# A two-layer linear-attention and MLP kernel: the first MLP block's layer norm scaled on ScalarE and turned through DRAM, six queries put off, constants moved to GpSimd

## The chip, the cores and the metric

The kernel runs on one core of one Trainium2 chip. The metric is the device time of one execution in microseconds (us); the profile's span is the part of an execution from the core's first to its last recorded instruction. Engines: PE is TensorE (PEld its weight loads), DVE is VectorE, ACT is ScalarE, POOL is GpSimd, SP is SyncE, which issues most DMAs here.

## What is computed

`x` has 2048 rows of 448 values. Two layers run one after the other with the same weights, and each adds a linear-attention block (16 heads of 28) and an MLP block to `x`:

```python
phi = lambda t: jnp.where(t > 0, t + 1, jnp.exp(t)) + 1e-6
def A(x):
    q, k, v = split(x @ wqkv)
    pq, pk = phi(q), phi(k)
    kv = einsum("bhsd,bhse->bhde", pk, v);  z = pk.sum(rows)
    o = einsum("bhqd,bhde->bhqe", pq, kv) / (einsum("bhqd,bhd->bhq", pq, z)[..., None] + 1e-6)
    return merge(o) @ wo
def B(x):
    return gelu_tanh(x @ w1 + b1) @ w2 + b2
x = x + A(layernorm(x)); x = x + B(layernorm(x))
x = x + A(layernorm(x)); x = x + B(layernorm(x))
```

`w1` is 448x1792, `w2` 1792x448. Everything is float32.

## The kernel before, in words

**Tiles.** The rows are cut into 16 tiles of 128, four tiles make a block. A matrix product is done in two halves: each operand is split into a rounded part and the rest (hi and lo, type fp32r), and hi·hi, hi·lo and lo·hi are accumulated in PSUM. A query or key projection of one tile (Q, K) is therefore eleven matmuls into one bank; so is `f`, the first MLP product of 128 of the 1792 columns for a whole block; `y` is the second one, four `u` (one per tile) of three matmuls.

**Order.** Nothing is scheduled at run time. The string ORDER lists operations as short tokens (`Q10` is query projection of tile 10, `:m` or `:acc` names a bank or an engine, `>` marks an operation of the next layer done early); each token emits its instructions, and every engine works through its own instructions in that order. SP's DMAs too go out in that order; a DMA also waits for the one that was issued eight before it. So the order of the string is the order of every queue.

**Layer norm.** `a` and `la` take a tile's mean and variance on DVE and add 1e-5 (`bve`); `ar` raises that to -0.5 on POOL (`brs`); `n` and `ln` scale the tile on DVE (line 361). The result must be transposed before a product over its 448 columns. There are two ways: on PE (`T`, `mT`: four transposes against an identity, line 390, into one bank), or *in squares*: DVE transposes 32x32 squares (`tu`, `pu`, `mu`, lines 398 and 399), the half block of two tiles is stored to DRAM (`st`, `ps`, `ms`, line 404) and read back with four loads that put the squares in place (`sp`, `pp`, `mp`, line 410). Either way ACT then casts the hi part (`xh`, `qh`, `yh`) and DVE subtracts to get lo (`xl`, `ql`, `yl`). Before the change the first MLP block of each layer (tiles 0 to 3, `ln lx mT yh yl`) goes through PE, the other three blocks in squares (`ln mu ms mp yh yl`).

**Attention.** Keys run first: `K`, phi (`ke` on ACT, `kp` on DVE), hi and lo (`kh`, `kl`), the sum over rows `za`, and `G` = xnᵀ·phi(k), four banks. Queries (`Q qe qp`) are stored to DRAM (`qs`) and read back later (`pl`), since their denominators need the sum over all keys. After the last G: `z` and `zb` (the key sum on all partitions), `dc` (its 1e-6 share per head), `gt` (G to SBUF), `kv`, `mask`, and `m`: four products with `wo` (hi `mh`, lo `ml`). Per query tile: `pz` multiplies by zb on POOL, `pd` sums per head, adds dc and inverts on DVE, `pm` scales; for tiles 0 to 3 `pT` turns on PE, and `o`, `oa`, `la` add the attention to the tile and take its statistics. `oc` does the same for the later tiles, in between the MLP's `f` and `y`.

**MLP.** `f` (PE), `g` (gelu, ACT), `gh` (ACT) and `gl` (DVE), `y` (PE), at the end of a block `ya` (DVE) and `ys` (DMA out). `lb` adds b2 on POOL.

**Around the change.** In layer 0 PE's order after the key phase was: K15 G13 G14 z G15 Q11 kv pT1 Q12 m3 pT0 m0 m1 m2 pT3 o0 pT2 o1 o2 mT0 o3 Q13 mT1 mT2 Q14 mT3 Q15 f0; in layer 1: K15 G13 G14 G15 Q10 z kv Q11 m0 m1 m3 pT1 m2 pT0 Q12 o0 pT2 o1 pT3 o2 mT0 o3 mT1 Q13 mT2 Q14 mT3 Q15 f0. At the layer boundary: f54 f55 y50 y51 y52 y53 y54 K0 y55 Q0 K1 Q1 G0 (K0 on, of layer 1).

PSUM has eight banks: four `acc` (G, then m, o, then y), two `h` (T, Q, f), two `m` (K, z, kv, pT, mT, oc).

## Time and profile before

| | us |
|---|---|
| median of 3 runs | 879.77 |
| lowest, highest | 879.72, 881.26 |
| the profiled execution, its whole time | 879.86 |
| its span | 878.1 |
| granted clock of TensorE, mean | 0.999 |

In the rows below, a group row reads: line, engine, operation, out<-in with shapes, count | busy us, mean ns of one | idle time of the engine just before them and what ended most of it. A row of the chain or a timeline begins with its start and its duration in us. Matmuls are pipelined: a matmul's duration is longer than the distance to the next one's start, so PE's work is counted by starts.

### The profile page before, as it was taken

How to read it: one execution, taken by the hardware profiler on the slowest of the kernel's cores; microseconds unless marked ns; L12 is line 12 of the kernel's file. 1: busy time of each engine (PE TensorE's matmuls, PEld its weight loads, DVE VectorE, ACT ScalarE, POOL GpSimd, SP SyncE). 2: the span in 40 equal slices, each digit the busy share in tenths (PEclk: the TensorE clock that was granted, in tenths of full speed). 3: DMA queues.
4: the chain of work that ended last, by engine and by line, in shares of the span. 5: the costliest groups of instructions: out<-in, count | busy, mean ns of one | idle time of the engine just before them, and what ended most of it. 6: DMA issues, size and time to landing. Idle time of an engine off the chain costs nothing.

```text
span 878.1 us, 11548 instructions
## 1 busy us (share of the span) xinstructions
PE 872.7 (99%) x4181; PEld 772.6 (88%) x4181; DVE 473.4 (54%) x972; ACT 336.4 (38%) x596; POOL 202.5 (23%) x239
## 2 busy tenths in 40 slices
PE   9999999999999999999999999999999999999998
PEld 7999988889888888888889898988888888888887
DVE  7886587357574343324378765954572743343112
ACT  6777634332323221424255653333233132223221
POOL 4665543123132011010023233130220220130000
PEclk9999999999999999999999999999999999999999
DMA  6575732541713124221064452333125142120101
GB/s 210 175 238 175 215 95 104 166 117 58 221 50 117 43 68 119 63 84 49 24 204 161 138 182 84 95 125 98 66 87 166 46 119 86 37 96 5 38 1 43
DMA packets 62762, 93.71 MB, mean 107 GB/s; under 512 B 8816, under 2 KB 57968, under 8 KB 62704
## 3 DMA queue, kind: packets, MB, share of 16 engines
q1 hardware_dynamic: 62400, 92.51, 33.3%
q8 instruction: 33, 0.54, 0.3%
q10 hardware_dynamic: 304, 0.46, 0.2%
q14 instruction: 25, 0.20, 0.1%
HBM read 55.65 MB, written 34.08 MB: 102 GB/s over the span
## 4 chain that ended last, share of the span: by engine, by line
PE 97%; DVE 1%; DMA 1%; ACT 0%; POOL 0%; SPq 0%; issue 0%; ACTq 0%; POOLq 0%
PE y L878 10%; PE y L877 10%; PE y L879 10%; PE hp L851 9%; PE hp L852 9%; PE hp L850 9%; PE hp L854 3%; PE hp L853 3%; PE G L618 2%; PE G L619 2%; PE G L617 2%; PE psq L543 2%; PE psq L545 2%; PE psq L544 2%; PE psk L543 2%; PE psk L544 2%
## 5 line engine op out<-in xcount | busy, mean ns | idle before, releaser
L869 DVE TENSOR_TENSOR gl<-g,gh 128x512 fp32r<-128x512 f32 x112 | 79.8, 720 | 193.8 <-ACT gh L211 193.5
L859 ACT ACTIVATE g<-hp,b1s 128x512 f32<-128x512 f32 x112 | 76.3, 688 | 228.8 <-PE hp L854 210.4
L878 PE MATMUL y<-w2l,gh 128*128 128x448 f32 x448 | 163.7, 365 | 0.0
L877 PE MATMUL y<-w2h,gh 128*128 128x448 f32 x448 | 163.6, 365 | 0.0
L879 PE MATMUL y<-w2h,gl 128*128 128x448 f32 x448 | 163.6, 365 | 0.0
L851 PE MATMUL hp<-XH,w1l 128*128 128x512 f32 x336 | 131.2, 391 | 0.0
L852 PE MATMUL hp<-XL,w1h 128*128 128x512 f32 x336 | 131.1, 390 | 0.0
L850 PE MATMUL hp<-XH,w1h 128*128 128x512 f32 x336 | 131.1, 390 | 0.0
L211 ACT CAST gh<-g 128x512 fp32r<-128x512 f32 x112 | 69.1, 620 | 155.6 <-PE y L878 144.1
L357 POOL TENSOR_TENSOR brs<-bve,mhalf 128x1 f32<-128x1 f32 x64 | 41.0, 642 | 318.9 <-DVE bve L351 318.9
L877 PEld LDWEIGHTS y<-w2h,gh 128*128 128x128 f32 x448 | 84.1, 188 | 8.3
L878 PEld LDWEIGHTS y<-w2l,gh 128*128 128x128 f32 x448 | 84.1, 188 | 7.9
L879 PEld LDWEIGHTS y<-w2h,gl 128*128 128x128 f32 x448 | 84.2, 188 | 6.6
L852 PEld LDWEIGHTS hp<-XL,w1h 128*128 128x128 f32 x336 | 63.1, 188 | 13.6
L851 PEld LDWEIGHTS hp<-XH,w1l 128*128 128x128 f32 x336 | 63.1, 188 | 11.9
L850 PEld LDWEIGHTS hp<-XH,w1h 128*128 128x128 f32 x336 | 63.1, 188 | 11.8
L716 POOL TENSOR_TENSOR pz<-pq,zb 128x448 f32<-128x448 f32 x32 | 37.8, 1184 | 70.2 <-DVE dn L721 43.6
L535 POOL TENSOR_TENSOR xnl<-x,xnh 128x384 fp32r<-128x384 f32 x32 | 33.7, 1052 | 81.6 <-ACT xnh L211 81.5
L428 DVE TENSOR_TENSOR XL<-sp,XH 128x512 fp32r<-128x512 f32 x50 | 36.7, 748 | 23.3 <-ACT XH L211 23.3
L795 DVE TENSOR_TENSOR x<-op,x 128x448 f32<-128x448 f32 x32 | 19.8, 618 | 49.3 <-PE op L789 48.5
L853 PE MATMUL hp<-XH,w1x 128*128 128x512 f32 x112 | 43.6, 389 | 0.0
L854 PE MATMUL hp<-XL,w1x 128*128 128x512 f32 x112 | 43.6, 389 | 0.0
(162 smaller groups left out, 1572.7 us busy)
## 6 DMA issues: line engine op xcount, KB each, us to landing
x<-in_A_x_dram SPq DMA_DIRECT2D x32, 224.0 KB, 4.0
pq_d<-eq SPq DMA_DIRECT2D x32, 224.0 KB, 2.8
pq<-pq_d SPq DMA_DIRECT2D x32, 224.0 KB, 3.2
x<-x_d SPq DMA_DIRECT2D x32, 224.0 KB, 3.8
sq_a<-sq SPq DMA_DIRECT2D x13, 512.0 KB, 3.0
sp<-sq_a SPq DMA_DIRECT2D x52, 128.0 KB, 3.0
sq_q<-sq SPq DMA_DIRECT2D x12, 512.0 KB, 2.9
sp<-sq_q SPq DMA_DIRECT2D x48, 128.0 KB, 3.2
```

The source lines that it names most:

```text
L211: act.copy(out, src)
L357: pool.tensor_tensor(rs, ve, mhalf, op=OP.pow)
L850: pe.matmul(o, w1h[:, c, s], x.moving(x.hi, c), start=(c == 0), stop=False)
L851: pe.matmul(o, w1l[:, c, s], x.moving(x.hi, c), start=False, stop=False)
L852: pe.matmul(o, w1h[:, c, s], x.moving(x.lo, c), start=False, stop=False)
L853: pe.matmul(o, w1x[:, s], x.moving(x.hi, 3), start=False, stop=False)
L854: pe.matmul(o, w1x[:, s], x.moving(x.lo, 3), start=False, stop=True)
L859: act.activation(T[l, "g", n], T[l, "hp", n], AF.Gelu_apprx_tanh, bias=b1s[:, n % NF:n % NF + 1])
L869: dve.tensor_sub(lo, T[l, "g", n], f(hi))
L877: pe.matmul(o, gh[:, r], w2h[:, i, s], start=first, stop=False)
L878: pe.matmul(o, gh[:, r], w2l[:, i, s], start=False, stop=False)
L879: pe.matmul(o, gl[:, r], w2h[:, i, s], start=False, stop=last)
```

## The change

For both layers:

- The first MLP block no longer goes through PE: `lx` and `mT` are gone, tiles 0 to 3 get `mu`, `ms`, `mp` like the others.
- All sixteen `ln` per layer run as `ln:a`: DVE makes -mean·root (128x1), ACT scales with it as bias and with the root as scale.
- The 1e-5 is added on POOL in `ar`, not on DVE in `a`.
- `pz` leaves room for a 29th value per head, a new `pc` copies `dc` there on POOL, and `pd` is one sum and one reciprocal.
- The hi parts of `m` lie in the rings of kh and kl (E and F), not in S; some rings are wider, a padding constant goes.
- The order is new throughout. After the key phase of layer 0 PE has: K15 G13 G14 G15 z Q8 kv pT0 Q9 m2 m0 m1 m3 pT2 pT1 o0 o1 pT3 o2 o3 Q10 Q11:m Q15 Q12:acc Q13:acc Q14:m f0 f1 f5 u2 f2 u3 u1 u0 f4; of layer 1: K15 G13 G14 G15 z kv Q10 m1 pT0 m0 m2 m3 pT1 pT2 o0 o1 pT3 o2 o3 Q9 Q12 Q11:m Q15:acc Q14:m Q13:acc f0 f1 f3 u3 u0 f5 u1 u2 y1. The phi of some put-off queries (qe14; qe11, qe13, qe14) now follows g0 or g1. At the boundary: y52 f54 y53 y54 y55 K0 Q1 K1 Q0 G0 K2 G1 Q2 K3 Q3 G2 (K0 on, of layer 1).

```diff
-        "ld0 a0 ar0 ld1 a1 n0 hot16 wkld0 wkld1:a wkld2 wkld3:a wkh1 wkl1 ht0 wkh0 ar1 wkl0 n1 d0 ht1 hx0 hl0 hk0 "
-        "wkh2 wkl2 wkh3 d1 ht3 hx1 hl1 wqld0 wqh0 ht2 hx2 wkl3:p hk1 hx3 hl2 hk2 hl3 wql0 hk3 ld2 wqld1 wqh1 a2 "
...
-        "oa0 qp11 qs11 qh2 bhi23 blo23 la0 o1 ql2 o2 oa1 ar0 ln0 lx0 mT0 bhi24 qh3 bhi22 la1 ql3 o3 oa2 yh0 ar1 "
-        "blo22 la2 ln1 yl0 lx1 Q13 mT1 pz4 ar2 qe12 oa3 qp12 ln2 lx2 mT2 Q14 la3 ar3 yh1 yl1 ln3 qe13 qp13 lx3 "
-        "bld25:W5 qs10 yh2 pd4 yl2 qe14 qp14 qs12 mT3 yh3 yl3 bhi25 blo25 pl5 pz5 Q15 qe15 qp15 qs14 qs15 qs13 "
...
+        "ld0 hot16 a0 ld1 a1 ar0 n0 ht0 wkld0 wkld1:a wkld2 wkld3:a wkh1 wkl1 wkh0 wkl0 d0 ar1 n1 hx0 hl0 wkh3 "
+        "wkl3:p wkh2 wkl2 ht1 hx1 hk0 d1 hl1 ht2 hx2 ld2 a2 hl2 ht3 hx3 wqld0 wqld1 wqh1 wqh0 hl3 wql0 hk1 ke0 "
...
+        "bhi22 qe9 qh1 pm3 ql1 o0 qh2 bld25:W5 pl5 qs7 pl4 ld5 oa0 la0 ql2 o1 oa1 la1 bhi25 pT3 qh3 blo20 blo22 "
+        "ar0 ln0:a ql3 ar1 ln1:a o2 mu0 mu1 oa2 la2 ar2 o3 oa3 qp9 la3 ar3 ln2:a pz4 pc4 bld24:W6 pl6 ms0 mp0 "
+        "ln3:a mu2 mu3 ms1 qs9 bld21:xn Q10 Q11:m Q15 mp1 qe10 yh0 yl0 qp10 qs10 qe11 qp11 pd4 Q12:acc yh1 qe15 "
+        "qp15 ld4 qs15 pl7 yl1 yh3 yl3 yh2 yl2 Q13:acc qe13 qp13 qs13 qe12 qp12 qs12 Q14:m bld23:xn f0 g0 gh0 "
+        "bhi21 gl0 pm4 f1 f5 pz5 mc pc5 pd5 pm5 g1 gh1 pu4 gl1 u2 f2 u3 u1 bhi23 u0 qe14 g2 gh2 pu5 ps2 pp2 qs11 "
...
-        ve = small(1, "bve")
-        dve.tensor_scalar(ve, mv[:, 1:2], 1e-5, None, op0=OP.add)
-        return mv, ve
+        return mv, None
 
     def root(key):
-        mv, ve = T[key]
-        rs = small(1, "brs")
-        pool.tensor_tensor(rs, ve, mhalf, op=OP.pow)
+        mv, _ = T[key]
+        rs = small(3, "brs")
+        pool.tensor_scalar(rs[:, 0:1], mv[:, 1:2], 1e-5, None, op0=OP.add)
+        pool.tensor_tensor(rs[:, 1:2], rs[:, 0:1], mhalf, op=OP.pow)
         T[key] = mv, rs
 
-    def norm(out, xs, mv, rs):
-        dve.tensor_scalar(out, xs, mv[:, 0:1], rs, op0=OP.subtract, op1=OP.mult)
+    def norm(out, xs, mv, rs, e=None):
+        if e == "a":
+            dve.scalar_tensor_tensor(rs[:, 2:3], mv[:, 0:1], -1.0, rs[:, 1:2], op0=OP.mult, op1=OP.mult)
+            act.activation(out, xs, AF.Identity, bias=rs[:, 2:3], scale=rs[:, 1:2])
+        else:
+            dve.tensor_scalar(out, xs, mv[:, 0:1], rs[:, 1:2], op0=OP.subtract, op1=OP.mult)
...
-        T["pz", l, t] = ring(e or f"W{4 if t > 3 else 4 + t % 2}", D, "pz")
-        pool.tensor_tensor(T["pz", l, t], T["pq", l, t], T[l, "zb"], op=OP.mult)
+        s = ring(e or f"W{4 if t > 3 else 4 + t % 2}", D + H, "pz")
+        s = T["pz", l, t] = s.rearrange("p (h d) -> p h d", d=DH + 1)
+        pool.tensor_tensor(s[:, :, :DH], T["pq", l, t].rearrange("p (h d) -> p h d", d=DH),
+                           T[l, "zb"].rearrange("p (h d) -> p h d", d=DH), op=OP.mult)
+
+    @op
+    def pc(l, t, e):
+        pool.tensor_copy(T["pz", l, t][:, :, DH], T[l, "dc"])
 
     @op
     def pd(l, t, e):
         dn = small(H, "dn")
-        dve.tensor_reduce(dn, T["pz", l, t].rearrange("p (h d) -> p h d", d=DH), axis=AX.X, op=OP.add)
-        dve.tensor_tensor(dn, dn, T[l, "dc"], op=OP.add)
+        dve.tensor_reduce(dn, T["pz", l, t], axis=AX.X, op=OP.add)
         rd = T["rd", l, t] = small(H, "rd")
         dve.reciprocal(rd, dn)
```

More of the change, by code (lines that the diff above doesn't have):

```diff
@@ L161, in ring, with wide @@
         return work.tile([128, n], dt, name=name, tag=tag, bufs=BUFS.get(tag, 1))
+    def wide(tag):
+        return 512 if tag == "xn" else D + H if tag in ("W4", "W5") else D
     def small(n, name):
@@ L188, in linear_attn_mlp_kernel @@
     b2b = consts.tile([128, D], F32, name="b2b")
-    consts.tile([128, 48], F32, name="pad")
     w1h = wts.tile([128, 3, F], F32R, name="w1h")
@@ L261, in wpiece @@
     def wpiece(name, i):
-        return ring(f"{'W' if name == 'k' else 'V'}{i}", D, f"w{name}{i}", F32R)
+        tag = f"{'W' if name == 'k' else 'V'}{i}"
+        return ring(tag, wide(tag), f"w{name}{i}", F32R)[:, :D]
     def wload(name, col):
@@ L447, in n @@
         xs = T["xn", l, t] = T["x", l, t]
-        norm(xs, xs, *T["st", l, t])
+        norm(xs, xs, *T["st", l, t], e)
     @op
@@ L678, in mh @@
     def mh(l, g, e):
-        if g % 2 == 0:
-            T[l, "Mb", g // 2] = [ring("S", 1024, n, F32R) for n in ("Mh", "Ml")]
-        T[l, "Mh", g], T[l, "Ml", g] = (s[:G, g % 2 * D:(g % 2 + 1) * D] for s in T[l, "Mb", g // 2])
+        T[l, "Mh", g] = ring("EEFF"[g], 512, "Mh", F32R)[:G, :D]
         copy(ENG[e or "a"], T[l, "Mh", g], T[l, "mp", g])
@@ L685, in ml @@
     def ml(l, g, e):
+        if (l, "Mb", g // 2) not in T:
+            T[l, "Mb", g // 2] = ring("S", 1024, "Ml", F32R)
+        T[l, "Ml", g] = T[l, "Mb", g // 2][:G, g % 2 * D:(g % 2 + 1) * D]
         dve.tensor_sub(T[l, "Ml", g], T[l, "mp", g], f(T[l, "Mh", g]))
```

4 lines of the change are left out of this document (2 added, 2 removed), and 172 rows, old and new, of the table ORDER.

## The prediction

> **What bounds the kernel now.** I read the page first (busy times, chain), then what TensorE (PE) waits for, then the chain in order of time, then single timelines.
>
> ```profile
> span 878.1 us, 11548 instructions
> ...
> PE 872.7 (99%) x4181; PEld 772.6 (88%) x4181; DVE 473.4 (54%) x972; ACT 336.4 (38%) x596; POOL 202.5 (23%) x239
> ...
> PE 97%; DVE 1%; DMA 1%; ACT 0%; POOL 0%; SPq 0%; issue 0%; ACTq 0%; POOLq 0%
> ```
>
> PE is busy for 872.7 of 878.1 us and makes 97% of the chain; no other engine passes 54%. So the end is set by how many matmuls PE issues and by how seldom it stops. Two of the four stops that the view of PE's waits lists, in us, times, longest:
>
> ```profile
> PE G L618 <- DVE kl L580: 0.4, 1, 0.4
> PE tp L465 <- ACT tail L211: 0.3, 1, 0.3
> ```
>
> The first is at the layer boundary (G of layer 1 waits for kl), the second in the first ten microseconds. There is almost no idle time to win; time can only come out of PE's work, or go into new stops.
>
> **The change part by part.** *PE's removed work.* Each mT is four transposes of 128x128; eight mT go, so 32 matmuls. In the chain in order of time (start, us, what) they stand as
>
> ```profile
> 128.06 0.44 PE tp L390 x4
> 133.18 0.89 PE tp L390 x8
> 136.34 0.50 PE tp L390 x4
> ...
> 560.21 0.44 PE tp L390 x4
> 563.09 0.44 PE tp L390 x4
> 565.79 0.44 PE tp L390 x4
> 568.47 0.44 PE tp L390 x4
> ```
>
> 0.44+0.89+0.50+4x0.44 = 3.59 us. Behind a group of transposes PE also loses a little. In PE's timeline around another such group (start, duration):
>
> ```profile
> 113.95 0.45 PE L543 MATMUL psq<-wq,XH 128*128 128x448 f32 x1
> 114.24 0.37 PE L544 MATMUL psq<-wq,XH 128*128 128x448 f32 x1
> ...
> 116.06 0.36 PE L548 MATMUL psq<-wq,XL 128*128 128x448 f32 x1
> ```
>
> From 114.24 to 116.06 nine starts follow at 0.202 us each; the first one behind the transposes (113.95) takes 0.29, so 0.085 more. Seven groups: 0.6. PE's gain is 3.59+0.6 = 4.2 us. All other matmuls stay, in another order: the same Q, K, G, f, y, o, oc. A query projection is eleven matmuls, 11 x 0.202 = 2.23 us.
>
> *What takes the place of mT: a round trip through DRAM.* For the first MLP block each layer now stores two more half blocks (sq_m) and spreads them with eight loads on SP's queue. The last half sits on a serial path from o3 to f0: oa3, qp9 (layer 0 alone has it in between on DVE), statistics, the added epsilon and root on POOL, the bias on DVE, the scaling on ACT, mu3 on DVE, store, loads, two casts on ACT, one subtraction on DVE. Rows (count | busy, mean ns | idle before):
>
> ```profile
> L795 DVE TENSOR_TENSOR x<-op,x 128x448 f32<-128x448 f32 x32 | 19.8, 618 | 49.3 <-PE op L789 48.5 <-PE op L776 0.8
> L558 DVE SCALAR_TENSOR_TENSOR eq<-psq,eq 128x448 f32<-128x448 f32 x32 | 19.7, 616 | 3.5 <-ACT eq L554 3.4
> L347 DVE BATCH_NORM_STATS2 bst<-x 128x6 f32<-128x448 f32 x64 | 39.5, 617 | 4.9 <-DMA x<-in_A_x_dram 4.3 <-DMA x<-x_d 0.3
> L349 DVE BATCH_NORM_AGGREGATE bmv<-bst 128x2 f32<-128x6 f32 x64 | 11.7, 182 | 2.2
> L351 DVE TENSOR_SCALAR bve<-bmv 128x1 f32<-128x1 f32 x64 | 9.8, 154 | 2.2
> L398 DVE STREAM_TRANSPOSE sq<-xm 128x384 f32<-128x384 f32 x24 | 13.4, 560 | 0.2
> L399 DVE STREAM_TRANSPOSE sq<-xm 128x128 f32<-128x128 f32 x24 | 6.4, 268 | 0.0
> L428 DVE TENSOR_TENSOR XL<-sp,XH 128x512 fp32r<-128x512 f32 x50 | 36.7, 748 | 23.3 <-ACT XH L211 23.3
> ...
> L576 ACT ACTIVATE kh<-psk,tiny 128x448 fp32r<-128x448 f32 x32 | 20.2, 632 | 15.8 <-DVE psk L558 11.2 <-DVE za L589 4.5
> L211 ACT CAST XH<-sp 128x512 fp32r<-128x512 f32 x50 | 29.8, 614 | 12.2 <-DMA sp<-sq_m 6.3 <-DMA sp<-sq_a 5.8
> ...
> L357 POOL TENSOR_TENSOR brs<-bve,mhalf 128x1 f32<-128x1 f32 x64 | 41.0, 642 | 318.9 <-DVE bve L351 318.9
> L536 POOL TENSOR_TENSOR xnh<-x,xnh 128x64 fp32r<-128x64 f32 x32 | 12.0, 376 | 0.0
> ```
>
> No row shows an add of 128x1 on POOL: above it lies the root (642, same size), below it nothing; I take 0.38, the small POOL row. The scaling on ACT is an Identity of 128x448 like L576, 0.63 (from below the cast of 128x512, 0.61). Counted from the last matmul of o3: 0.4 until DVE may start, oa 0.62, qp9 0.62, statistics 0.80, add 0.38, root 0.64, bias 0.15, scaling 0.63, mu3 0.83: 5.1 us. Then SP's queue and the landing, from another half block in the old trace:
>
> ```profile
> 254.31 0.32 SPq L404 DMA_DIRECT2D sq_m<-sq  x1
> 256.89 1.74 SPq L410 DMA_DIRECT2D sp<-sq_m  x4
> ...
> sp<-sq_m SPq DMA_DIRECT2D x48, 128.0 KB, 2.9
> ```
>
> 256.89-254.31 = 2.6 for the store; the fourth load is issued 1.3 later (1.74 for four) and lands in 2.9: 6.8 us. So data at 11.9, the last cast (2x0.61) at 13.1, the last XL at 13.9. (Neighbours on one engine overlap a little and hand-offs cost a little; I set one against the other.)
>
> The cover is what the change puts off: six Q instead of three between o3 and f0, 6x2.23 = 13.4, so f0 can start at 13.6; it first reads XL in its third matmul, about 0.45 later, 14.05. In layer 0 the trip is covered with 0.15 to 0.5 to spare; in layer 1, without qp9, with 0.8. Three Q (6.7) would have left 7 us open. Queued behind the waiting loads on SP are the stores of the put-off queries and the next pq loads, which nobody needs soon; on ACT and DVE behind the casts stand qe13, qe12, qp13, qp12, whose banks are first wanted by f and u later. Since other transfers run at the time, I add 0.4 in layer 0 and 0.1 in layer 1; bounds 0 and 2.6, 0 and 2.1 (rival A has the row).
>
> *Work that moves off the path.* DVE loses 64 adds of 154 ns, 32 short adds of dc and the norms of the MLP, and gets eight more turns at 0.83 and 32 biases; ACT gets 32 scalings, 20 us in all, at 38% busy; POOL gets 64 small adds (at most 64x0.64 = 41 us) and 32 copies of 16 columns (0 to 0.38 each) at 23%. Their cover is PE, 99% busy. Without that cover they would cost what stands on the path: one add and one copy per tile in pd, under 1 us.
>
> *Shorter cover before o0 in layer 1.* Between kv and o0 stood Q11 and Q12; now only Q10.
>
> ```profile
> L721 DVE TENSOR_REDUCE dn<-pz 128x16 f32<-128x448 f32 x32 | 19.4, 605 | 1.8 <-POOL pz L716 1.8
> L729 DVE SCALAR_TENSOR_TENSOR pq<-pq,rd 128x448 f32<-128x448 f32 x32 | 26.2, 822 | 0.3
> L686 DVE TENSOR_TENSOR Ml<-mp,Mh 112x448 fp32r<-112x448 f32 x8 | 4.6, 614 | 0.1
> ...
> 117.62 2.26 PE mp L675 x6
> ```
>
> DVE's queue from the end of kv to ml2: mask (about 0.6), three pd (0.6, and a short reciprocal at 0.25 taken from L399), three pm (0.82), ql0 (0.7), four ml (0.61): 8.8 us. PE meanwhile: Q10 2.23, eight m matmuls at 2.26/6 = 3.0, three pT 1.3, then seven matmuls of o0 until Ml2 is read, 1.4: 8.0. Late by 0.8 at most, nothing if neighbours overlap; I take 0.4, range 0 to 1.0. Layer 0 keeps Q8 and Q9 there: nothing.
>
> *Start and boundary.* d1, on which PE waited 0.3 above, moves behind one more cast on ACT, and the root of tile 0 gets POOL's add (0 to 0.64): +0.3, range -0.3 to +1.2. At the boundary K, Q and G of layer 1 move up into layer 0's tail: the 0.4 stop may go, or a load of x in the DVE queue may stop G again: 0, range -0.5 to +1.5.
>
> **The sum**, against the profiled execution (879.86, of which 878.1 span; the median of the runs is 879.77, the same): -4.2 +0.4 +0.1 +0.4 +0.3 = -3.0, so 876.9 us.
>
> **A rule against the change.** The queries that are put off past f0 bring exp between the gelus: each MLP's opening now has a switch of ACT's table to exp and back, four more loads in all. ACT's timeline at the old switch:
>
> ```profile
> 442.17 0.55 ACT L553 ACTIVATE ek<-psk 128x448 f32<-128x448 f32 x1 [1.28 <-PE psk L548]
> 442.73 1.28 ACT L554 ACT_TABLE_LOAD   x1
> 444.02 0.58 ACT L554 ACTIVATE ek<-ek 128x448 f32<-128x448 f32 x1
> ...
> 139.53 0.23 PE hp L852
> ```
>
> A switch costs 1.28 and nothing around it: 2.6 us of ACT per layer. In layer 0, f4 needs the bank that g2 reads. From f0's start PE has f0, f1, f5, u2, f2, u3, u1, u0 ahead of it, 12.5 us (eleven starts of 0.23 for an f, three of 0.2 for a u); f2 ends at 10.7. On ACT g1 can start at 5.2, when f1 is done; g1, gh1, a w2 cast, relu and exp at about 0.6 each (the cast above) and two loads end at 10.8, and g2 at 11.5: 1.0 to spare. So nothing is added. [...]
>
> **The rivals.** *A, slower: the trip is longer than six queries cover.* For it: a load of this kind has taken
>
> ```profile
> q1 hardware_dynamic: 62400, 92.51, 33.3%
> ...
> 441.08 4.99 DMA sp<-sq_a
> ```
>
> in a busy stretch, 2.1 more than the 2.9, and here w2 pieces, x and pq share the queue. Against: the half block at 254.31 ran undisturbed, and the queue's packets take 33.3% of the engines' span on average. If store and last load both take 2.1 more, each layer's f0 stops for 4.2 less its spare (0.15, 0.8): 7.5 in all, 879.9-4.2+0.7+7.5 = 883.9. It decides from about 3 us more per trip. Chance 0.10. [...]
>
> *B, no change: the orders are stiffer.* ln on ACT stands in order ahead of gh and waits for a root on POOL that is later by the add; the same for pd behind the copy on POOL. If each of the 24 ln behind the first blocks costs 0.1, 2.4 us: 879.3. For it: both layers' orders are new throughout. Against: PE is ahead of y by two or three f, 2.5 us each. Chance 0.12.
>
> [...] Chance 0.05.
>
> *D, faster still: every new wait is covered and the boundary's stop goes:* 879.9-4.2-0.4 = 875.3. Chance 0.20. That the transposes were hidden anyway has no ground: they are in the chain.
>
> **How the numbers follow.** Forecast 0.53 (875.5 to 878.5 by its own terms), A 0.10, B 0.12, C 0.05, D 0.20. About 0.2%, 1.8 us, can be told from no change here. Faster: the forecast but for 0.03 of it and D, and a little of B: 0.72; same: B, C and the tail of the forecast: 0.17; slower: A and 0.01: 0.11. The range reaches from below D (874.6) past B and C and into the start of A, 881.0.
>
> **What would show it.** Right: 32 matmuls fewer, PE busy about 868 to 870, no L390 rows on xm, casts of XH from sq_m ending before Q13 or Q14 ends, PE's waits under 2 us in all. Wrong: PE waiting for XH or XL ahead of f0 by more than 1 us in either layer (A), for gh or gl in the MLP (B), for g2 behind a table load (C), for Ml ahead of o0 or for kl at the boundary by more than their ranges. The whole forecast falls if PE's busy time does not drop by about 4 us.

## The result, and the profile after

| | before | after |
|---|---|---|
| median, us | 880.35 | 892.38 |
| lowest, highest, us | 879.72, 881.26 | 891.57, 893.43 |
| the profiled execution, whole time and span, us | 879.86, 878.1 | 893.43, 891.4 |

The changed kernel takes 1.0137 times as long (95% interval 1.0119 to 1.0154). It is 12 us slower, where 3 us faster was forecast, and lies outside the range. The page of the profile after (span, engines, shares of the chain that ended last):

```profile
span 891.4 us, 11594 instructions
...
PE 878.4 (99%) x4149; PEld 768.9 (86%) x4149; DVE 452.4 (51%) x884; ACT 363.8 (41%) x632; POOL 228.8 (26%) x335
...
PE 78%; DVE 9%; DMA 4%; ACT 4%; issue 2%; POOL 2%; SPq 1%; ACTq 0%; DVEq 0%; POOLq 0%
```

The 32 transposes are gone (4181 matmuls before, 4149 now). Yet PE is busy for 878.4 us instead of 872.7, and its share of the chain fell from 97% to 78%. The prediction had named this as what would overthrow it: PE's busy time did not drop by 4 us, it rose by 5.7. So there are two losses: matmuls that run slower, and stops. PE's waits after (what PE waited for; us in all, times, longest):

```profile
PE hp L866 <- ACT XH L217: 2.9, 2, 2.0
PE y L893 <- ACT gh L217: 1.6, 1, 1.6
PE psk L553 <- DVE za L599: 1.5, 1, 1.5
...
PE tp L475 <- ACT tail L217: 0.3, 1, 0.3
```

Only the first row had a term in the sum; a wait for gh was named as the sign of rival B. The second row lies in the MLP of layer 1, the third in its key phase; in both a cast on ACT waits for a load and holds up what stands in order behind it.

To see all of it I counted in the traces, for every matmul, by how much the distance to the next start exceeds the usual pace of its kind (0.203 us for 448 columns, 0.227 for 512, 0.109 for a transpose, and so on). The work at these paces is 870.5 us before and 867.0 after, so 3.5 less (32 transposes at 0.109). The excess over it, us, by stretches of the run:

```
                        before   const      mT    wide   after   place  allplace
0-120   keys, start       0.6     0.9     3.9     3.0     3.2     0.2     3.8
120-160 ahead of f0       0.2     0.6     0.1     2.5     3.9     0.1     5.3
160-440 MLP, layer 0      0.2     0.6     0.8     1.6     3.0    -1.6     0.4
440-520 layer boundary    1.1     1.1     0.1     1.3     0.3    -0.2    -0.1
520-560 K, attention      0.3     0.4     3.2     2.5     3.1     0.1     2.2
560-600 ahead of f0       0.2     0.2     0.3     1.3     1.5     0.2     3.8
600-end MLP, layer 1      0.2     0.2     0.1     2.1     4.5    -1.5    -0.4
sum                       2.9     4.0     8.4    14.3    19.5    -2.7    15.0
```

(The kernels between the outer two are the experiments below; the stretches are those of the clock, so that a few tenths can fall to a neighbour. Each column is one execution, and executions of one order differ: counted alike, the run pz below, whose queues are those of after, has 2.7 less than after.) Before to after: -3.5 of work, +16.6 of excess, so 13.1 of the 13.3 by which the span grew. Where the excess arises is seen in three stops and in the pace.

**The stop ahead of f0 in layer 0.** Timeline of all engines after (start, duration, engine, line; in brackets the idle time before and who ended it):

```profile
129.56 1.16 POOL L728 TENSOR_TENSOR pz<-pq,zb 128x448 f32<-128x448 f32 x1
129.63 1.11 DVE L368 SCALAR_TENSOR_TENSOR brs<-bmv,brs 128x1 f32<-128x1 f32 x1 [1.02 <-POOL brs L363]
...
130.83 0.76 ACT L369 ACTIVATE xm<-x,brs 128x448 f32<-128x448 f32 x1 [1.37 <-DVE brs L368]
...
132.42 0.34 SPq L414 DMA_DIRECT2D sq_m<-sq  x1
132.80 0.43 SPq L615 DMA_DIRECT2D pq_d<-eq  x1
133.33 0.67 SPq L320 DMA_DIRECT2D stg<-in_B_w_dram  x1
...
135.02 1.75 SPq L420 DMA_DIRECT2D sp<-sq_m  x4
...
140.38 1.14 ACT L217 CAST XH<-sp 128x512 fp32r<-128x512 f32 x2 [3.27 <-DMA sp<-sq_m]
...
141.57 0.51 PE L866 MATMUL hp<-XH,w1h 128*128 128x512 f32 x1 [1.98 <-ACT XH L217]
```

o3's last matmul starts at 126.02. The prediction had the store 5.1 us later; it came 6.4 later. 1.0 of these 1.3 is one instruction: the bias of tile 3, 128x1, which was taken at 0.15, took 1.11, and it ends together with the product pz of 448 columns that POOL had begun 0.07 before it. Without pz beside it the same instruction took 0.16 (run pz2 below). From store to the casts it took 8.0 where 6.8 was reckoned. The loads were issued 2.6 behind the store, as reckoned; from there to the cast it took 5.4 instead of 4.2. Why is not shown: with the same queue it took 4.4 in the run pz below, and from 4.4 to 5.4 in this place in six profiles that have the trip (pz, all, wide, pz2, lnd, after). So the last cast ended at 141.5 (13.1 after o3 forecast, 15.5 measured), while the six queries ended at 139.6. PE stopped for 1.98 us.

Then something follows that no wait shows. Windows of after (columns: from:to, length, busy time and count of PE, PEld, DVE, ACT, POOL, then the granted clock, DMA share, GB/s):

```profile
138.00:140.00 2.00, 1.59 (x8) 1.14 (x7) 0.36 (x1) 0.00 (x0) 0.00 (x0) 1.00 0.94 270
140.00:142.00 2.00, 0.43 (x2) 0.30 (x2) 0.97 (x2) 1.59 (x4) 0.00 (x0) 0.98 0.68 252
142.00:144.00 2.00, 2.00 (x6) 1.33 (x5) 1.31 (x3) 1.57 (x3) 0.00 (x0) 0.50 0.01 3
144.00:146.00 2.00, 2.00 (x8) 1.58 (x7) 0.27 (x1) 0.75 (x1) 0.00 (x0) 0.66 0.73 245
```

PE is busy without a gap from 142 to 146, but at clock 0.50 and 0.66: (1-0.50)x2 + (1-0.66)x2 = 1.7 us lost, almost as much as the stop itself; it is one stretch of 3.4 us at 0.50. This belongs to the busy time that rose. It is not in every execution: of the changed kernel's four runs, the two at mean clock 1.000 took 892.1 and 891.57, those at 0.998 and 0.999 took 893.43 and 892.67. A stop of 1.98 us stands ahead of this fall; the repeat pz below, with 1.0 in this place, kept 1.00. (More on it in the last section.)

**The stop in the MLP of layer 1**, from the timeline after:

```profile
723.72 3.92 SPq L420 DMA_DIRECT2D sp<-sq_m  x8
...
728.48 0.62 ACT L217 CAST XH<-sp 128x512 fp32r<-128x512 f32 x1 [3.24 <-DMA sp<-sq_m]
731.34 1.14 ACT L217 CAST XH<-sp 128x512 fp32r<-128x512 f32 x2 [2.24 <-DMA sp<-sq_m]
...
732.38 0.68 ACT L875 ACTIVATE g<-hp,b1s 128x512 f32<-128x512 f32 x1
733.09 0.62 ACT L217 CAST gh<-g 128x512 fp32r<-128x512 f32 x1
```

ACT stood still for 3.24 and 2.24 us ahead of casts of a later block whose loads were on their way, with g26 and gh26 in order behind them; PE's y, which needs gh26, waited 1.6. **The stop in the key phase of layer 1** is the same thing:

```profile
522.53 1.74 SPq L420 DMA_DIRECT2D sp<-sq_a  x4
...
527.27 0.62 ACT L217 CAST XH<-sp 128x512 fp32r<-128x512 f32 x1 [2.24 <-DMA sp<-sq_a]
...
527.79 0.63 ACT L586 ACTIVATE kh<-psk,tiny 128x448 fp32r<-128x448 f32 x1
...
529.06 0.61 DVE L599 TENSOR_TENSOR za<-psk,za 128x448 f32<-128x448 f32 x1
...
529.82 0.44 PE L553 MATMUL psk<-wk,XH 128*128 128x448 f32 x1 [1.55 <-DVE za L599]
```

xh14 stands ahead of kh12 on ACT and waits 2.24 for its load, so kh12 is late, za12 is late, and the bank of K is free 1.55 too late.

**The pace.** First and last of 60 matmuls in a row of y, and of f in a row, in PE's timelines of before (59 and 43 distances) and after (59 and 54):

```profile
410.14 0.39 PE L850 MATMUL hp<-XH,w1h 128*128 128x512 f32 x1
...
419.92 0.39 PE L854 MATMUL hp<-XL,w1x 128*128 128x512 f32 x1
...
427.58 0.36 PE L877 MATMUL y<-w2h,gh 128*128 128x448 f32 x1
...
439.54 0.36 PE L879 MATMUL y<-w2h,gl 128*128 128x448 f32 x1
```
```profile
646.08 0.36 PE L893 MATMUL y<-w2h,gh 128*128 128x448 f32 x1
...
658.11 0.36 PE L895 MATMUL y<-w2h,gl 128*128 128x448 f32 x1
658.31 0.40 PE L866 MATMUL hp<-XH,w1h 128*128 128x512 f32 x1
...
670.69 0.40 PE L870 MATMUL hp<-XL,w1x 128*128 128x512 f32 x1
```

y went from 11.96/59 = 0.2027 to 12.03/59 = 0.2039 us per matmul, f from 9.78/43 = 0.2274 to 12.38/54 = 0.2293, with no wait anywhere in these stretches and the clock at 1.00. The instructions are the same; what differs is where their operands lie, and the runs wide and shift below test that. The change widens two rings (W4, W5) by 64 bytes each and drops a padding constant, and all that is allocated behind them moves.

### The profile page after: what moved, and what is told of

It is laid out like the page before. It is cut to its first block, busy times and chain, and to the rows that moved or that the text cites. A ratio compares the mean times of both kernels' runs of the same rounds, so it can differ in the third digit from the quotient of the medians.

```text
span 891.4 us, 11594 instructions
## 1 busy us (share of the span) xinstructions
PE 878.4 (99%) x4149; PEld 768.9 (86%) x4149; DVE 452.4 (51%) x884; ACT 363.8 (41%) x632; POOL 228.8 (26%) x335
## 4 chain that ended last, share of the span: by engine, by line
PE 78%; DVE 9%; DMA 4%; ACT 4%; issue 2%; POOL 2%; SPq 1%; ACTq 0%; DVEq 0%; POOLq 0%
PE y L894 9%; PE y L893 9%; PE y L895 9%; PE hp L868 8%; PE hp L866 8%; PE hp L867 8%; PE hp L869 3%; PE hp L870 3%; PE op L803 2%; PE op L801 2%; PE op L802 2%; PE G L628 1%; PE G L629 1%; PE G L627 1%; PE psk L553 1%
## 5 line engine op out<-in xcount | busy, mean ns | idle before, releaser
L362 POOL TENSOR_SCALAR brs<-bmv 128x1 f32<-128x1 f32 x64 | 17.2, 269 | 324.6 <-DVE bmv L356 241.1
L438 DVE TENSOR_TENSOR XL<-sp,XH 128x512 fp32r<-128x512 f32 x58 | 43.5, 765 | 25.6 <-ACT XH L217 25.6
L830 POOL TENSOR_TENSOR x<-x,b2b 128x448 f32<-128x448 f32 x32 | 40.1, 1270 | 17.0 <-ACT xm L369 17.0
L217 ACT CAST XH<-sp 128x512 fp32r<-128x512 f32 x58 | 34.0, 613 | 24.3 <-DMA sp<-sq_m 16.5
```

The source lines that it names most:

```text
L217: act.copy(out, src)
L438: dve.tensor_sub(squares(lo), spread_tile(kind, l, t), f(squares(hi)))
L830: (ENG[e or "p"]).tensor_tensor(T["x", l, t], T["x", l, t], b2b, op=OP.add)
```

## The experiments

Each time below stands beside runs of the kernel before on the same chip; the ratio is to these, in brackets its 95% interval.

### First four: addresses, the bias, the clock, the casts

**wide** gives W4 and W5 512 floats each, so that what lies behind them is back where it was, modulo 256 bytes, and changes nothing else:

```diff
-        return 512 if tag == "xn" else D + H if tag in ("W4", "W5") else D
+        return 512 if tag in ("xn", "W4", "W5") else D
```

> The changed kernel with the rings W4 and W5 2048 bytes wide instead of 1856, so that every work tile starts at a multiple of 256 bytes again, as in the kernel before; nothing else differs. Theory 'addresses': the starts of f and y lie 0.2296 and 0.2037 us apart in the changed kernel, 0.2279 and 0.2027 in the kernel before, because of where the tiles lie; the old pace comes back (f 0.228, y 0.2027, G 0.203 instead of 0.205, but Q 0.203 instead of 0.200) and the time falls by 2 to 3 us, to about 890. Rival 'not the addresses' (order of the instructions, the chip of that day): the distances stay within 0.0005 of the changed kernel's and the time within 1 us of 892.4.

889.11 us, 1.0106 (1.0091 to 1.0121): 3 us less than after. The excess in the two MLP stretches fell from 3.0 and 4.5 to 1.6 and 2.1. The stops stayed, though shorter in this profile: 1.1 ahead of f0 in layer 0, 1.0 in the keys, 1.0 for gh. So the excess alone cannot tell pace from stops; the paces in shift below do.

**pz** moves the product that held the bias behind the store, in the order string of layer 0:

```diff
-  ar3 ln2:a pz4 pc4 bld24:W6 pl6 ms0 mp0 ln3:a mu2 mu3 ms1 qs9
+  ar3 ln2:a bld24:W6 pl6 ms0 mp0 ln3:a mu2 mu3 ms1 pz4 pc4 qs9
```

> The changed kernel with one token pair moved: in layer 0 the product pz4 and its copy pc4 on GpSimd stand behind the second store ms1 instead of behind ln2. Theory 'held up by GpSimd': the bias of tile 3's layer norm on DVE took 1.11 us instead of 0.15 because the 1.16 us product ran on GpSimd at the same time; it falls to 0.15, the store leaves 0.9 to 1.0 earlier and f0's stop of 2.1 us falls to 1.1 to 1.3; if the short stop no longer lowers the clock (0.50 at 142 to 144 us), another 1.8 go: 890.5 to 889.5. Rival 'coincidence': the bias still takes about 1.1 us or the loads land no earlier, stop and time as in the changed kernel (892.4).

892.33 us, 1.0141 (1.0124 to 1.0158), and the bias still took 1.10. The edit was empty: between the two places no other instruction of GpSimd stands, so its queue is unchanged. The run is a repeat of the changed kernel, and tells nothing of the bias. As a repeat it shows how far the stops vary with no change of any queue:

```profile
PE hp L866 <- ACT XH L217: 2.0, 2, 1.0
```

That is 1.0 ahead of f0 in each layer, with the clock at 1.00 throughout, where the profile of after has 2.0 and 0.9. The stops in the keys and for gh are 1.3 and 1.2 here, 1.5 and 1.6 there.

**hot** puts ten matmuls ahead of f0 in layer 0 whose result nobody reads, so that PE does not stop:

```diff
-  bld23:xn f0 g0
+  bld23:xn hot10:h f0 g0
```

> The changed kernel with ten idle matmuls of ones (128x512) on PE ahead of f0 in layer 0, in the bank of f1; they fill the stop of 2.1 us and compute nothing that is used. Theory 'clock': the eight matmuls behind the stop ran at half pace because the granted clock fell to 0.50 after it; with PE kept busy the clock stays at 1.00, f0 starts at 141.4 to 141.7 as before and the next ten starts lie 0.23 apart: 1.6 to 2.0 us less, 890.5. Rival 'slow for another reason' (the casts and loads that run at the time, XL coming late): the same slow starts behind f0, time 892.4 to 893.

891.26 us, 1.0125 (1.0108 to 1.0142). Windows of hot:

```profile
138.00:142.00 4.00, 4.00 (x20) 3.49 (x19) 1.51 (x4) 1.42 (x3) 0.00 (x0) 1.00 0.91 282
142.00:144.00 2.00, 2.00 (x10) 1.47 (x9) 1.30 (x3) 1.75 (x4) 0.00 (x0) 1.00 0.04 13
```

Ten f matmuls in the 2 us from 142 instead of six, at clock 1.00: with the stop filled the clock did not fall, in this profile. The gain in the median, 1.1, is no more than the measurement can tell, since the clock fell in some of after's runs only. One thing more is seen in this profile: PE does not wait for gh in the MLP of layer 1, where no token was moved; a stop of 0.9 for another gh appears in layer 0.

**cast** moves, in layer 1, the casts that waited for loads behind the instructions that PE needs:

```diff
-  xh14 kp12 kh12 G11 sh12 xh15 sh13 sl12 sl13 xl14 kl12 za12
+  kp12 kh12 xh14 G11 sh12 xh15 sh13 sl12 sl13 kl12 za12 xl14
...
-  mp5 yh8 yh10 pm13 pu13 yh11 yl10 yl8 ps6 pl15 g26 gh26 gl26 y25 y26 pp6 yl11
+  mp5 pm13 pu13 ps6 pl15 g26 gh26 gl26 yh8 yh10 y25 y26 pp6 yh11 yl10 yl8 yl11
```

> The changed kernel with casts moved in layer 1's order: xh14 behind kh12 and xl14 behind za12; yh8, yh10, yh11, yl10 and yl8 behind gl26. Theory 'a cast that waits for a load holds ScalarE's queue': PE's stops at 527.9 (1.7 us, psk behind za) and 731.8 (1.7, y behind gh, 0.7 more just after) go, 3 to 4.4 us less: 888.0 to 889.4. Rival 'the loads are late, whoever waits': the stop moves to K14 or to f29 in the same size, time within 1 us of 892.4.

889.06 us, 1.0105 (1.0090 to 1.0120). The row for psk and za is gone, and the y stop fell from 1.6 to 0.6 (now for gl). Excess from 520 to 560: 3.1 to 1.6; 600 to the end: 4.5 to 2.7. Together the moves are worth about 3 us, uncertain by 2. That the stop in the keys is an in-order cast ahead of needed work is shown: it stands in all seven profiles with the tokens of after in this place (1.0 to 1.7), and in none of the four where they are moved (this one, kfix, all, allplace). For the y stop it is likely, not shown: it shrank here, but it is also 0.4 in lnd and absent in hot, where this place was not touched.

### The change taken apart

**const** is the kernel before with the constants on GpSimd alone (1e-5 in `ar`, `pc`, one sum in `pd`); the order is that of before, with each pc ahead of its pd, the addresses are those of before modulo 256, ln is on DVE, mT on PE:

```diff
-  pz4 ... pd4
+  pz4 ... pc4 pd4
```

> The order of the kernel before, with only the constants moved: the added epsilon of the variance and the copy of the denominators' constant (pc, next to each pd) are on GpSimd, and W4 and W5 are 2048 bytes wide so that every work tile starts at a multiple of 256 bytes. Transposes, norms on DVE and three put-off queries stay. Theory 'the new orders cost it, not these parts': GpSimd's adds and copies are hidden, 879.5 to 880.8. Rival 'constants on GpSimd lengthen each chain' (an add of 0.27 us ahead of each root, a copy of 0.21 ahead of each reciprocal, in both attentions and MLPs): new stops of PE behind x tiles and pq, 882 to 885.

881.43 us, 1.0014 (1.0006 to 1.0022): 1.2 us.

**pz2** is wide, with pl4, pz4 and pc4 of layer 0 behind ms1 and pd4 behind yl2, so that GpSimd's product really comes later:

```diff
-  o0 qh2 bld25:W5 pl5 qs7 pl4 ld5 ... ln2:a pz4 pc4 bld24:W6 pl6 ms0 mp0 ln3:a mu2 mu3 ms1 qs9
+  o0 qh2 bld25:W5 pl5 qs7 ld5 ... ln2:a bld24:W6 pl6 ms0 mp0 ln3:a mu2 mu3 ms1 pl4 pz4 pc4 qs9
```

> The changed kernel with 2048-byte W4 and W5 (as in the run wide) and, in layer 0, the load pl4 with pz4 and pc4 behind the store ms1 and pd4 behind the last XL. In the run pz GpSimd's own queue had not changed and the bias still took 1.10 us; here pz4 cannot start before the store. Theory 'held up by GpSimd': the bias takes 0.15, the store leaves 0.9 to 1.0 earlier against o3 (5.4 instead of 6.4 us behind o3's last matmul), f0's stop of 1.1 to 2.1 falls to 0 to 1.1 and the clock stays at 1.00: 887 to 888.3 beside 889.1 of wide. Rival: the load lands when the queue lets it, stop and time as in wide.

888.12 us, 1.0089 (1.0076 to 1.0101). DVE's timeline of pz2:

```profile
129.66 0.16 DVE L368 SCALAR_TENSOR_TENSOR brs<-bmv,brs 128x1 f32<-128x1 f32 x1 [1.02 <-POOL brs L363]
```

0.16 instead of 1.11, so the product was the cause, and the store left 0.9 earlier. But from store to casts it now took 8.0, where wide had 7.3: with pl4's load between them the last loads were issued 3.0 behind the store instead of 2.6, and the rest is within what the same queue varies by. f0's stop only went from 1.15 to 0.89.

**mT** is wide with the first block turned on PE again (for tiles 0 to 3 lx and mT, no mu, ms, mp); all else, the ACT scaling and the new orders too, as in after:

```diff
-  o3 oa3 qp9 la3 ar3 ln2:a pz4 pc4 bld24:W6 pl6 ms0 mp0 ln3:a mu2 mu3 ms1 qs9 bld21:xn Q10 Q11:m Q15 mp1
+  o3 oa3 mT0 Q10 qp9 la3 ar3 ln2:a lx2 mT1 ln3:a lx3 Q11:acc yh0 yl0 yh1 yl1 Q15 mT2 mT3 yh2 yl2 yh3 yl3
```

> The changed kernel with 2048-byte W4 and W5 (as in the run wide), the first MLP block of each layer turned by PE's 32 transposes again (lx, mT; no mu, ms, mp), three or four of the put-off queries around them; the rest of the order, ScalarE's scaling and the constants on GpSimd stay. Theory 'the swap itself is worth its 4.2 us less what f0 waits': PE gets 3.6 of transposes and 0.6 of restarts, f0's stops (layer 0: 1.3 to 4.0, layer 1: 0.9 to 1.5, with their slow starts) go; 889 to 891, within 1.5 us of wide, and the stops in K (1.3), the attention (1.1) and layer 1's second block (2.0) stay. Rival 'the swap is what lost the time' (its loads crowd the queue and its store and casts hold DVE and ScalarE everywhere): with the transposes the time falls under 886.

885.88 us, 1.0063 (1.0051 to 1.0076): the rival's side. In this order the trip through DRAM, the thing that the change is named for, costs more than the transposes it saves: 1.0106-1.0063 = 0.0043, 3.8 us net, uncertain by about 1.7. The excess shows how: wide has 5.9 more (14.3 against 8.4), of it 2.4 and 1.0 ahead of f0 and 2.0 in the MLP of layer 1, against 3.5 of saved work; that is 2.4 net in these two profiles. The y stop goes too, which may tie it to the trip; as it was absent in hot, which has the trip, this is not shown. The longest stop that stays in mT, from its waits:

```profile
PE psk L553 <- DVE za L599: 1.7, 1, 1.7
```

**lnd** is wide with the scaling back on DVE (`:a` dropped from every ln):

```diff
-  ln0:a ql3 ar1 ln1:a
+  ln0 ql3 ar1 ln1
```

> The changed kernel with 2048-byte W4 and W5 (as in the run wide) and the 32 layer norms of the MLP on DVE (one subtract-and-multiply of 0.4 to 1.0 us) instead of a bias on DVE and a scaling of 0.76 us on ScalarE. Theory 'ScalarE's scaling adds a hop to the trip': the store of tiles 2 and 3 leaves 0.4 to 0.9 earlier, f0's stops fall by as much, 888 to 888.8 beside 889.1. Rival 'the norm is as long held up on DVE by GpSimd's product as the bias was': within 0.5 us of wide.

888.71 us, 1.0093 (1.0080 to 1.0106), against wide's 1.0106 (1.0091 to 1.0121): the scaling on ACT costs nothing that can be told here. (All four runs of lnd show a mean clock of 0.998, three of wide's four 1.000; the fall of the clock in after cost 1.7 us, so lnd may have gained up to that much elsewhere.) The place of the norm on DVE does not save the trip, since it too is held by pz, 1.33 against a median of 0.51 over the 32 (DVE's timeline of lnd):

```profile
130.63 1.33 DVE L370 TENSOR_SCALAR xm<-x,bmv,brs 128x448 f32<-128x448 f32 x1 [0.77 <-POOL brs L362]
```

### Addresses, a shorter trip, one more stop

**shift** is the kernel before with after's addresses:

```diff
     def ring(tag, n, name, dt=F32):
+        if tag in ("W4", "W5"):
+            return work.tile([128, n + 16], dt, name=name, tag=tag, bufs=BUFS.get(tag, 1))[:, :n]
```

> The kernel before, with the rings W4 and W5 64 bytes wider, so that the tiles behind them start where they start in the changed kernel modulo 256 bytes (XH, XL, wk0 and wk2 at 64, kh, kl, gh, gl, xnh and wq at 128); order and instructions are those of the kernel before. Theory 'addresses': f goes from 0.2279 to 0.2296 us between starts, y from 0.2027 to 0.2037, G from 0.203 to 0.205, Q from 0.203 to 0.200, and the time rises by 2 to 3.5 us, to 882 to 884. Rival 'it was the order or those runs': distances and time stay (within 0.0005 and 0.7 us of the kernel before).

883.30 us, 1.0037 (1.0024 to 1.0049): 3.3 us slower by 64 bytes twice, with no instruction changed. It agrees with the 3 us that wide took out of after. The paces came as well: y 0.2041 in a row of 60, f 0.2289.

**half** is the kernel before with only tiles 0 and 1 through DRAM, in an order written by hand:

```diff
-  ln0 lx0 mT0 ... ln1 lx1 Q13 mT1
+  ln0 mu0 ... ln1 mu1 ms0 ... o3 mp0
```

> The kernel before (its order, three put-off queries, norms and constants on DVE) with only tiles 0 and 1 of each first MLP block turned by squares and tiles 2 and 3 by PE: 16 transposes fewer. The round trip starts with o1 instead of o3, so o2, o3, three queries and eight transposes (some 13 us) cover its 7 us from store to landing. Theory 'what cost the time was the late half and the re-planned order': no stop ahead of f0 over 0.5 us, 1.8 of transposes and 0.3 of restarts less, 877.5 to 878.8 where the kernel before has 880. Rival 'any half block by squares loses what it saves' (the casts and the store hold DVE, ScalarE and SP elsewhere): 880 to 883, with stops ahead of f0 or in the first f and y.

893.82 us, 1.0156 (1.0142 to 1.0169). This order is bad by itself. In layer 1 PE waits 6.2 us for the norm of tile 3: on DVE it stands behind the phi of Q13, whose part on ACT waits for the store of an earlier query, which I put behind two loads of x:

```profile
578.71 0.54 ACT L554 ACTIVATE eq<-psq 128x448 f32<-128x448 f32 x1 [12.37 <-DMA pq_d<-eq]
```

In layer 0 PE waits 2.0 for ql. One of those two loads, that of tile 2's x, stands behind the addition of the attention's sum, so that the kernel leaves that sum out for tile 2 of layer 1. The run does not answer whether half a trip is worth having.

**kfix** is mT with the key phase mended, kl5 moved up in layer 0 and the casts of layer 1 as in cast:

```diff
-  sh5 sh6 kh5 qe4 qp4 ... za6 kl5 kh6
+  sh5 sh6 kh5 kl5 qe4 qp4 ... za6 kh6
```

> The run mT with three tokens moved in the K stages: kl5 behind kh5 in layer 0, xh14 behind kh12 and xl14 behind za12 in layer 1. Theory 'the re-planned K stages wait behind casts and other tiles' work': the stops at 524 (1.85 us) and 75 (0.6) go, 883.2 to 884.2 beside 885.9 of mT. Rival 'with fewer queries in the K stage PE has to wait somewhere': the stops move to the next K and the time stays within 0.7 us of mT.

885.53 us, 1.0063 (1.0047 to 1.0078). The stop of 1.7 is gone from the waits (the row psk <- za is no more), the excess from 520 to 560 fell from 3.2 to 2.1, and the span of the profiled run from 883.7 to 882.6. In the ratio none of it can be seen. A stop of 0.5 that kl5 was to take away stayed.

### All repairs at once, and the law of addresses

**all** is pz2 with the moves of cast and kfix, and with a single query store left in SP's queue between the half block's store and its loads:

```diff
-  ms1 pl4 pz4 pc4 qs9 bld21:xn Q10 Q11:m Q15 qe10
+  ms1 qs9 mp1 pl4 pz4 pc4 bld21:xn Q10 Q11:m Q15 qe10
```

> The changed kernel with every repair that the runs so far point to: 2048-byte W4 and W5 (wide); in layer 0 pl4, pz4, pc4 and bld21 behind the loads mp1, pd4 behind the last XL, kl5 behind kh5; in layer 1 pl5 and pz5 behind mp1, xh14 behind kh12, xl14 behind za12, and yh8, yh10, yh11, yl8 and yl10 behind gl26 (cast). Theory 'the parts add up': 889.1 of wide less 3.3 of cast, less 0.5 to 1.5 of the two store paths: 884.3 to 885.3; what is left above the kernel before is f0's stops (1 to 1.5 in all) and the small stops of layer 0's K stage and of the attentions. Rival 'a removed stop returns at the next place': 887 or more.

886.59 us, 1.0071 (1.0059 to 1.0084) and so above what was expected. The stops in K and y are gone or small, but f0 now waits 1.0 for XL in each layer (DVE and POOL in the timeline of all):

```profile
138.69 2.24 DVE L438 TENSOR_TENSOR XL<-sp,XH 128x512 fp32r<-128x512 f32 x2 [2.06 <-ACT XH L217]
139.06 1.32 POOL L728 TENSOR_TENSOR pz<-pq,zb 128x448 f32<-128x448 f32 x1 [9.96 <-DMA pq<-pq_d]
```

The two subtractions took 2.24, where wide's took 1.29: pz, moved out of the bias's way, landed on the last step of the same trip. The delay was moved, not removed. Beside kfix, 1.0063 (1.0047 to 1.0078), which keeps the transposes, all is no slower that could be told: with the orders mended the trip and the transposes come out alike, to within about 2 us. So the 3.8 us of mT belong to the trip in its old order.

**gap64, gap128, gap192** are the kernel before with gaps only. In each, w1 and w2 start d bytes further, modulo 256, and so do the rings from wq's on up to that of kh; all else lies as before:

```diff
-    consts.tile([128, 48], F32, name="pad")
+    consts.tile([128, d / 4 - 16], F32, name="pad")
...
     w2l = wts.tile([128, NF, D], F32R, name="w2l")
+    wts.tile([128, (256 - d) / 4], F32, name="gap1")
...
+    gaps = {"V": d / 4, "E": (256 - d) / 4}
```

> The kernel before with only places moved: w1, w2 (w1h to w2l) and the query weights wq start at 64 modulo 256 bytes, everything else at 0 as before. Theory 'what counts is how far the streamed operand's start lies from the weights' modulo 256': Q was fast (0.200) where wq lay 64 behind XH, so Q (wq at 64, XH at 0) and y (w2 at 64, gh at 0) now both take 0.200 instead of 0.203; 1344 and 352 matmuls, 4.4 us less, 875.5 to 877 if f does not lose. Rival 'each tile's own place counts' (64 or 128 is slow or fast whatever the other operand): y and Q not alike, or both at 0.203 or slower; 880 to 884.

> As gap64, with w1, w2 and wq at 128. Theory 'distance': y (w2 128 beyond gh) as y in the changed kernel, where gh lay 128 beyond w2: 0.204; Q the same, 0.204; 882 to 883. Rival 'own place': Q keeps the 0.200 that it had with wq at 128, and y with w2 at 128 as well: 876 to 877.

> As gap64, with w1, w2 and wq at 192. Theory 'distance': the streamed operand lies 192 (that is, -64) beyond the weights, which no kind has had here alone but part of K in the changed kernel (wk1 at 0, XH at 64; its distances were 0.2006 to 0.2066): between 0.200 and 0.207, no sign forecast. Rival 'own place': no forecast either; the run completes the four places.

882.28 (1.0025, 1.0016 to 1.0034), 886.82 (1.0074, 1.0061 to 1.0088) and 882.09 (1.0019, 1.0009 to 1.0028). The single products tell more than the sums. In PE's timeline of gap128:

```profile
413.41 0.40 PE L855 MATMUL hp<-XH,w1h 128*128 128x512 f32 x1
...
423.44 0.39 PE L859 MATMUL hp<-XL,w1x 128*128 128x512 f32 x1
...
431.23 0.37 PE L882 MATMUL y<-w2h,gh 128*128 128x448 f32 x1
...
443.27 0.36 PE L884 MATMUL y<-w2h,gl 128*128 128x448 f32 x1
```

With the start of the streamed operand less the start of the weights, modulo 256 bytes (in y the 448 columns of w2 stream against blocks of gh, in f the 512 columns of XH against blocks of w1), us per matmul:

| distance, bytes | y, 448 columns | f, 512 columns |
|---|---|---|
| 0 | 0.2027 (before) | 0.2274 (before) |
| 64 | 0.2002 (gap64) | 0.2293 (after), 0.2291 (gap192) |
| 128 | 0.2039 (after), 0.2041 (gap128) | 0.2333 (gap128) |
| 192 | 0.2022 (gap192) | 0.2333 (gap64) |

Wide, whose rings W4 and W5 are 256 bytes wider each than those of before, has the places of before modulo 256 alone, and y takes 0.2027 in both. Of the four, the best distance is 64 for 448 columns and 0 for 512; the queries keep to the column of y (0.2005, 0.2034 and 0.2020 in the three), less sharply: at distance 0 the mean distance between starts within a Q went from 0.2029 (all) to 0.2052 (kfix), while y and f stayed within 0.0002 over the eight profiles that have them at 0. In after y lay at 128 and f at 64, both off, and Q at 64, which alone gained.

### Two placed kernels

**place** is the kernel before with gaps chosen by this table, so that y, Q and K have distance 64 and f has 0:

```diff
-    consts.tile([128, 48], F32, name="pad")
...
+    wts.tile([128, 16], F32, name="gap0")
     w2h = wts.tile([128, NF, D], F32R, name="w2h")
...
+    gaps = {"XH": 48, "W2": 16, "E": 48}
```

> The kernel before with only places moved, so that the streamed operand starts 64 beyond the weights modulo 256 bytes wherever that was faster: XH, w1, kh and gh at 64, w2, wk and wq at 128 (f and G at distance 0, y, Q, K and the second-half sums oc at 64). Theory 'distance': y 0.2007, Q and K 0.200 to 0.2006 instead of 0.2027, f stays at 0.228: 1344 x 0.0019 + 704 x 0.0024 + 264 x 0.0022 = 4.8 us less, 875 to 876.5 beside 880.3. Rival 'those places of gap64 were special, not the distance': one of the kinds keeps its old pace or slows, 878 to 883.

874.31 us, 0.9935 (0.9922 to 0.9947): 6.2 us faster than before, and the fastest kernel of this study. Its page:

```profile
span 872.6 us, 11548 instructions
...
PE 867.3 (99%) x4181; PEld 771.3 (88%) x4181; DVE 471.5 (54%) x972; ACT 336.6 (39%) x596; POOL 203.6 (23%) x239
```

All 4181 matmuls, transposes included, and PE is busy 5.4 us less than before. y has 0.2002, f 0.2272, Q 0.2000.

**allplace** is all with its operands placed likewise:

```diff
+    wts.tile([128, 16], F32, name="gap0")
     w2h = wts.tile([128, NF, D], F32R, name="w2h")
...
+    gaps = {"XH": 32, "E": 48}
```

> The run all (the changed kernel with its repairs), with w2 and wq 64 beyond gh and XH, f at distance 0, instead of every tile at 0. Theory 'distance': 886.6 less 3.5 to 4.2, 882.4 to 883.1: the places help the changed kernel as much as the kernel before, and the change still costs 6 us beside place. Rival: what the places give is lost again in its stops, 885 or more.

885.85 us, 1.0056 (1.0040 to 1.0071): the rival's side. y got its 0.2001 and f 0.2271; the MLP stretches have an excess of 0.4 and -0.4 instead of all's 1.1 and 0.9. The stops around f0 ate it, from its waits:

```profile
PE hp L871 <- ACT g L880: 2.4, 2, 2.1
PE hp L871 <- ACT XH L222: 1.9, 2, 1.1
```

The 2.1 of the first row lies behind the first two f: in layer 0 a switch of ACT's table (1.28) stood behind a store for which ACT had waited 1.54, and g was 2.1 late. Behind this stop and behind layer 1's, the clock was at 0.50 (from 149.6 to 152.6 and from 579.9 to 582.5). (This profile is the slowest of the four runs, 888.95; the others took 885.0 to 886.5.) PE's waits for XH, XL and g add up to 5.3 us here and to 3.2 in the run without the placing. That a faster PE reaches f0 earlier and finds the trip as long as before is likely, not shown.

## Why the prediction was wrong, by its own steps

The step that failed is the cover. The sum took PE's work as nearly all that counts and put what the other engines do late at 1.2 in all, the new order of the keys and of the MLP at nothing; and it had no term at all for the addresses. In place of a gain the runs show 2.9 us for the addresses, 4.3 for the new orders, 3.8 net for the trip and 1.2 for the constants.

**PE's removed work, -4.2:** right in kind, 0.5 too large. At the usual paces 32 transposes are 3.5. The 0.6 of restarts was a misreading: behind five of the seven groups the next matmul starts 0.03 after the last transpose instead of 0.11, which gives back the 0.085 that it takes longer; the seven lose 0.2 together.

**The trip in layer 0, +0.4 with bounds 0 and 2.6:** the stop was 2.0, in the bounds and far from the value. The bias taken at 0.15 took 1.11, and store to cast took 8.0 for 6.8. The 0.15 was the mean of a row of the kernel before; I did not ask what POOL would run at that moment, though the order of the changed kernel has pz4 right there. What was not a term at all is the clock behind the stop, 1.7 in the profiled run. Hence 3.7 more excess ahead of f0 than before, in an execution with a long stop; the repeat pz had 1.0 and no fall.

**The trip in layer 1, +0.1 with bounds 0 and 2.1:** 0.9 of PE's 2.9 for XH, in the bounds. The store left 6.3 after o3's last matmul, where the same terms without qp9 give 4.5; here too a bias, that of tile 2, took 0.85 beside a product.

**o0 in layer 1, +0.4; start, +0.3; boundary, 0:** PE's waits after have no row for Ml, tail stands at 0.3 as before, and the boundary's stretch has 0.8 less excess. The first two are in their ranges, the boundary is 0.3 better than its range.

**Work that moves off the path, nothing:** for the scaling this held (lnd); for the constants on GpSimd it was 1.2 (const). But this step stood for the whole new order as well, with PE as its cover, and there it failed. PE was to hide what other engines do late; a cast on ACT that waits for a load (2.24 and 3.24 us in the rows above) blocks in order what PE needs next. Rival B came nearest, stiffer orders, but named the root and the copy on POOL and took 2.4 for 24 places at 0.1. Beside the y stop it was the key phase, for which the sum had no term: one stop of 1.0 to 1.7 in layer 1, and in layer 0 many under 0.7. From the ratios, mT less const, new orders and scaling: 1.0063-1.0014, 4.3 us.

**Rival C, 0.05 in the sum of the chances:** no run shows a table switch that costs more than its load. After has eight loads of 1.28; behind six of them ACT's next instruction starts 0.01 later, behind the other two it comes 0.46 and 1.94 later, and among PE's waits of after none is for g.

**Not in the prediction: the addresses, +3.** The diff showed rings getting wider and a padding constant going, and I told of it in the change, yet gave it no term.

The 12 us by ratios, with 880 us and each difference uncertain by 1 to 2 us:

| | from | us |
|---|---|---|
| addresses | after and pz, 1.0139, to wide, 1.0106 | 2.9 |
| DRAM trip for the transposes in this order, net | wide to mT, 1.0063 | 3.8 |
| orders, scaling on ACT, m's hi parts in other rings | mT to const, 1.0014 | 4.3 |
| constants on GpSimd | const to before | 1.2 |

The forecast missed by 15.5 us: these 12.2 and the 3 that it expected to gain. A single term of -4.2 stood on rows; the other side consisted of covers believed to hold. The stops ahead of f0 lie inside their bounds, but these were drawn for slower loads: half of the delay in layer 0 and nearly all of it in layer 1 arose before the store.

**What stays open.** Of the 4.3, only the stop in layer 1's keys was taken out by moving its tokens (cast, kfix), and in kfix the time did not fall by an amount that could be told; the 3 us that mT has over const in the first 120 us lie in many stops under 0.7 each, which no run takes out one by one. That const's order does not have them points to the order and not to the engines, but is no more than that. Why the last loads took 4.4 us in one execution and 5.4 in another from issue to cast is open too.

## What to carry to other kernels

When a change swaps work of the engine that bounds the kernel for a trip past three other engines, cost every step of the trip with what its neighbours run at that moment, and search each in-order queue for a waiting instruction ahead of one that the bounding engine needs. In a kernel that keeps TensorE 99% busy the starts of its operands are a tuning knob of their own: the kernel before gained 6.2 us by three gaps, more than the change could have saved at best. A diff that touches a buffer's size is to be read as a change of all addresses behind it: here 64 bytes twice, 3.3 us (shift).
